# Layer norm split between VectorE and GpSimd, and the attention residual in two later step parts

## The chip, the cores and the metric

The kernel runs on one core of a Trainium2 chip. A core has five instruction streams: TensorE (PE in the profile, with its weight loads listed as PEld), VectorE (DVE), ScalarE (ACT), GpSimd (POOL) and SyncE (SP, which issues DMAs here). Each stream runs in its own order; between streams there are only semaphores. The metric is the device time of one execution in microseconds (us).

## The reference

Two rounds of an attention layer A and a gated feed-forward layer B, with the same weights in both rounds, on 2048 tokens of width 448.

```python
x = A_x
x = x + _A_ref(_layernorm(x), A_mem0, A_Wq, A_Wk, A_Wv, A_Wo, A_seg_len)
x = x + _B_ref(_layernorm(x), B_W_gate, B_W_up, B_W_down)
x = x + _A_ref(_layernorm(x), A_mem0, A_Wq, A_Wk, A_Wv, A_Wo, A_seg_len)
x = x + _B_ref(_layernorm(x), B_W_gate, B_W_up, B_W_down)

def _layernorm(x, eps=1e-05):
    return (x - mean(x)) / sqrt(var(x) + eps)
```

`_A_ref` walks the tokens in 64 segments of 32. Each segment attends, with 16 heads of 256, to 8 memory tokens and to itself; the attention's output for the memory tokens is the memory of the next segment, so the segments form a chain. `_B_ref` computes gate = x Wg (kept where positive), up = x Wu and (gate * up) Wd, with 1792 hidden columns.

## The kernel before

The weights are combined first: for each head, A holds Wq Wk^T and B holds Wv Wo, both kept on chip in bf16. Then come 72 steps and one closing step. In a step one segment of the first round (chain 0) and one segment of the second round (chain 1, 8 segments behind) are computed together, so that their 2 x 40 columns share PE's weight loads. A tile is 128 tokens, four segments; a block is four steps, and g mod 4 tells where in its block a step stands.

What a step does on PE, in the order of the code (`step`):

1. `project` for the first eight heads, the transposes of the input (`kps`), `project` for the other eight. Each product `prj` is copied out of PSUM by DVE or ACT into TQ or TZ.
2. Scores: `Sm` (memory rows) and `Sx` (segment rows) for both halves. `weights_of` makes the softmax, on DVE except for the exponential on ACT; its last result is PM or PX.
3. `fill(0)`, then `project_out` in pieces (`ox`), between them the transposes of PM and PX (`pps`, copied by DVE into PT) and the products `ya`, `yb` and `y` of those with the input, whose evacuations write Y.
4. `fill(1)` stands before the second half's `project_out`, `fill(2)` after `weigh_x(0)`, and `fill(3)` after `finish`, which copies the new memory into hT (DVE, `set_mem`) and the attention output into OT (ACT).

A `fill(k)` emits what the table `slots` holds for slot 4g + k. There the layer norms and the feed-forward are put. For block gb, with slot 16 gb + 16 as its zero:

- slot 3: `residual` for both tiles of the block (one of each round). It transposes OT on PE (`otp`), adds it to the tile in x_ring (line 341) and makes the layer norms of both tiles together.
- slots 4 to 12: the 21 units of the feed-forward: `xposed` (transposes of the normalised tiles, `tps`, evacuated into xT), 14 `gate_up` and six thirds of `down`. The last third for the first tile also starts that tile's next norm; the last third for the second tile stores the tile and reloads its place in x_ring, with DMAs on SP.
- slot 14: `prep_pe(1, ...)` writes the first tile into hT for round two.
- slots 4 and 6 also hold the next tile's norm for round one, `prep_ln`, and its `prep_pe`.

The order of PE's products and transposes is fixed as they are emitted (`in_order`). On the other engines a list scheduler orders the instructions of each engine when the program is built; on the chip each engine keeps that order.

A layer norm before (`rstd_nbias`, `layer_norm`): on DVE bn_stats, bn_aggr, three small operations for a seed of the inverse root (lines 261 to 266), three rounds of four operations of 128x1 or 128x2 (lines 270 to 274) that refine it, and one for the bias; on ACT one activation of 128x448 per tile (line 285); on POOL a copy of the last 64 columns (line 287), so that the tile has 512. Two tiles of one residual share the small operations.

Of the kernel before, what the change touches and what calls it, by code (L numbers as in the profile page):

```python
# [8 lines left out]
BF = mybir.dt.bfloat16  # L9
F32 = mybir.dt.float32  # L10
I32 = mybir.dt.int32
AF = mybir.ActivationFunctionType
ALU = mybir.AluOpType
AX = mybir.AxisListType

DM = 448
# [10 lines left out]
EPS = 1e-5  # L27
# [17 lines left out]
def build_kernel(ctx, tc, A_x, A_mem0, A_Wq, A_Wk, A_Wv, A_Wo, B_W_gate, B_W_up, B_W_down, out,  # L45
                 ntiles=16, nseg=64):
    nc = tc.nc
    P = nc.NUM_PARTITIONS
# [9 lines left out]
    psum = ctx.enter_context(tc.tile_pool(name="psum", bufs=7, space=bass.MemoryType.PSUM))  # L58
    p_ln = ctx.enter_context(tc.tile_pool(name="p_ln", bufs=2))
# [14 lines left out]
    def tr(*a):  # L74
        in_order(nc.tensor.transpose(*a))  # L75
# [10 lines left out]
    def xsl(t):  # L86
        return x_ring[:, t % R, :]
# [3 lines left out]
    ident = glob.tile([P, P], BF, name="ident")  # L91
# [7 lines left out]
                            op0=ALU.arith_shift_right, op1=ALU.bitwise_and)  # L99
    nc.vector.tensor_scalar(out=rowi[:, 2:3], in0=rowi[:, 0:1], scalar1=15, scalar2=None,  # L100
                            op0=ALU.bitwise_and)
# [9 lines left out]
    for b in range(4):  # L111
        o = 0 if b % 2 == 0 else MEM
        nc.vector.tensor_scalar(out=maskS[:, b, o:o + SEG], in0=keyf[:, b // 2, :], scalar1=rowf[:, 2:3],
                                scalar2=MASKVAL, op0=ALU.is_gt, op1=ALU.mult)
# [4 lines left out]
                            op0=ALU.mult, op1=ALU.add)  # L119
# [5 lines left out]
    for i in range(2):  # L125
        t = glob.tile([P, 4, HW], BF, name=f"hT{i}")
# [5 lines left out]
    with tc.tile_pool(name="pre", bufs=6) as pre:  # L132
# [4 lines left out]
        for i in range(6):  # L137
            t = pre.tile([P, 4, 512], BF, name=f"nat{i}", bufs=1)
# [111 lines left out]
        HK.append(t)  # L250


    def rstd_nbias(ts):
        n = len(ts)
        mv = p_ln.tile([P, 2, 2], F32, tag="ln_mv")
        for i, t in enumerate(ts):
            stats = p_ln.tile([P, nc.vector.BN_STATS_DIM], F32, tag="ln_stats")
            nc.vector.bn_stats(stats[:], xsl(t))
            nc.vector.bn_aggr(mv[:, i, :], stats[:])
        veps = p_ln.tile([P, 2], F32, tag="ln_veps", name="ln_veps")[:, 0:n]  # L260
        nc.vector.tensor_scalar(out=veps, in0=mv[:, 0:n, 1], scalar1=EPS, scalar2=None, op0=ALU.add)
        ti = p_ln.tile([P, 2], I32, tag="ln_ti", name="ln_ti")[:, 0:n]
        nc.vector.tensor_scalar(out=ti, in0=veps.bitcast(I32), scalar1=1, scalar2=None,
                                op0=ALU.arith_shift_right)
        rstd = p_ln.tile([P, 2], F32, tag="ln_rstd", name="ln_rstd")[:, 0:n]
        nc.vector.tensor_scalar(out=rstd.bitcast(I32), in0=ti, scalar1=-1, scalar2=0x5f3759df,
                                op0=ALU.mult, op1=ALU.add)
        tmp = p_ln.tile([P, 2], F32, tag="ln_tmp", name="ln_tmp")[:, 0:n]
        for _ in range(3):
            nc.vector.tensor_tensor(out=tmp, in0=rstd, in1=rstd, op=ALU.mult)  # L270
            nc.vector.tensor_tensor(out=tmp, in0=tmp, in1=veps, op=ALU.mult)
            nc.vector.tensor_scalar(out=tmp, in0=tmp, scalar1=-0.5, scalar2=1.5,
                                    op0=ALU.mult, op1=ALU.add)
            nc.vector.tensor_tensor(out=rstd, in0=rstd, in1=tmp, op=ALU.mult)
        nbias = p_ln.tile([P, 2], F32, tag="ln_nbias", name="ln_nbias")[:, 0:n]
        nc.vector.scalar_tensor_tensor(out=nbias, in0=mv[:, 0:n, 0], scalar=-1.0, in1=rstd,
                                       op0=ALU.mult, op1=ALU.mult)
        return rstd, nbias

    def layer_norm(ts):  # L280
        rstd, nbias = rstd_nbias(ts)
        xns = []
        for i, t in enumerate(ts):
            xn = p_ln.tile([P, 512], BF, tag="ln_xn", bufs=3)
            nc.scalar.activation(xn[:, 0:DM], xsl(t), AF.Identity,
                                 bias=nbias[:, i:i + 1], scale=rstd[:, i:i + 1])
            nc.gpsimd.tensor_copy(xn[:, DM:512], xn[:, 384:DM])
            xns.append(xn)
        return xns

    def transpose_tokens(xn):
        tps = psum.tile([P, 4, 128], BF, tag="ps", name="tps")
# [5 lines left out]
        return hTb[b % 2][:].rearrange("p s (i w) -> p s i w", w=HI)  # L298

    def prep_ln(t):  # L300
        return layer_norm([t])[0] if 0 <= t < ntiles else None

    def prep_pe(c, t, xn):

        if xn is None:
            return
        b = t + (LAG // 4 if c else 0)
        tps = transpose_tokens(xn)
        src = tps[:].rearrange("p k (s t) -> p k s t", t=SEG)
        h = chunks(b)  # L310
        x = slice(HX[c], HX[c] + SEG)
        nc.vector.tensor_copy(h[:, :, 0:4, x].transpose([0, 2, 1, 3]), src)
# [12 lines left out]
    def ffn_units(gb):  # L325

        tasks = []
        if gb < ntiles:
            tasks.append((0, gb))
        if 0 <= gb - LAG // 4 < ntiles:  # L330
            tasks.append((1, gb - LAG // 4))
        n2 = 128 * len(tasks)
        pr = Pair()

        def residual():
            for c, t in tasks:
                tp = psum.tile([P, 4, 128], BF, tag="ps", name="otp")
                for kd in range(4):
                    tr(tp[:, kd, :], OT[:, c, kd, :], ident[:])
                xt = xsl(t)  # L340
                nc.vector.tensor_tensor(xt, tp[:].rearrange("p k d -> p (k d)")[:, 0:DM], xt, op=ALU.add)
            pr.xns = layer_norm([t for _, t in tasks])

        def xposed():
            pr.xT = main.tile([P, 4, 256], BF, tag="xT", name="xT")
            pr.hh = main.tile([P, FT, 256], BF, tag="hh", name="hh")
            for i, xn in enumerate(pr.xns):
                tps = transpose_tokens(xn)
                evac(nc.scalar if i == 0 else nc.vector, pr.xT[:, :, 128 * i:128 * i + 128], tps[:])

        def gate_up(f):
            gps = psum.tile([P, 512], F32, tag="ps", name="gps")
            ups = psum.tile([P, 512], F32, tag="ps", name="ups")
            for W_sb, ps in ((Wu_sb, ups), (Wg_sb, gps)):
                for kd in range(4):
                    mm(ps[:, 0:n2], W_sb[:, kd, f * 128:(f + 1) * 128], pr.xT[:, kd, 0:n2],
                                     start=(kd == 0), stop=(kd == 3))
            ut = p_ut.tile([P, 256], BF, tag="ut")
            nc.scalar.copy(ut[:, 0:n2], ups[:, 0:n2])  # L359
            nc.vector.scalar_tensor_tensor(out=pr.hh[:, f, 0:n2], in0=gps[:, 0:n2], scalar=0.0,  # L360
                                           in1=ut[:, 0:n2], op0=ALU.max, op1=ALU.mult)

        def down(i, part):
            c, t = tasks[i]
            if part == 0:
                pr.dps = psum.tile([P, 512], F32, tag="ps", name="dps")
            f0, f1 = ((0, 5), (5, 10), (10, FT))[part]
            for f in range(f0, f1):
                mm(pr.dps[:, 0:DM], pr.hh[:, f, 128 * i:128 * i + 128], Wd_sb[:, f, :],
                                 start=(f == 0), stop=(f == FT - 1))  # L370
            if part < 2:
                return
            xt = xsl(t)
            nc.vector.tensor_tensor(xt, pr.dps[:, 0:DM], xt, op=ALU.add)  # L374
            if c == 1:
                nc.sync.dma_start(out_dram[t * 128:(t + 1) * 128, :], xt)
                if t + R < ntiles:
                    nc.sync.dma_start(xsl(t + R), x_dram[(t + R) * 128:(t + R + 1) * 128, :])

        def down_last(i):  # L380
            down(i, 2)
            if tasks[i][0] == 0:
                pr.xn2 = prep_ln(gb)

        units = [xposed] + [lambda f=f: gate_up(f) for f in range(FT)]
        for i in range(len(tasks)):
            units += [lambda i=i: down(i, 0), lambda i=i: down(i, 1), lambda i=i: down_last(i)]
        post = (lambda: prep_pe(1, gb, pr.xn2)) if gb < ntiles else None
        return residual, units, post


    def moving(hb, j, idx, chains):
# [201 lines left out]
    def at(s, fn):  # L594
        slots.setdefault(s, []).append(fn)

    for gb in range(nsteps // 4):
        residual, units, post = ffn_units(gb)
        s0 = 4 * (4 * gb + 4) + 3
        at(s0, residual)  # L600
        first, last = s0 + 1, s0 + 10
        for i, u in enumerate(units):
            at(first + (i * (last - first)) // len(units), u)
        if post is not None:
            at(last + 1, post)
        if gb + 1 < ntiles:
            sl = Pair()
            at(4 * (4 * gb + 1), lambda sl=sl, t=gb + 1: setattr(sl, "xn", prep_ln(t)))
            at(4 * (4 * gb + 1) + 2, lambda sl=sl, t=gb + 1: prep_pe(0, t, sl.xn))

    prep_pe(0, 0, prep_ln(0))
    set_mem(0, mem0T[:].unsqueeze(2), (0,))
# [66 lines left out]
```

## Time and profile before

| what | value |
|---|---|
| median of 3 runs (lowest, highest) | 1897.17 us (1897.12, 1898.62) |
| the profiled execution: its time | 1896.18 us |
| its span, first to last instruction | 1894.4 us |
| mean granted PE clock | 0.973 |
| line 258, DVE bn_stats, 128x448, x64 | 616 ns each |
| lines 270, 271, 272, 274, DVE, 128x1, x108 each | 158, 153, 149, 155 ns each |
| line 285, ACT activation, 128x448, x64 | 757 ns each |
| line 312, DVE copy into hT, 128x512 bf16, x32 | 413 ns each |
| line 341, DVE add of the residual, x32 | 386 ns each |

A line of the page's groups reads: source line, engine, operation, result and operands with their shapes and count, then busy us in total, mean ns of one, and the idle time of the engine just before such instructions with what ended it. A line of the timeline reads: start, length, engine, source line, operation, operands, count of merged instructions, and in brackets the idle time before and the instruction that ended it. Since matmuls are pipelined, an idle time of PE is a better measure of a wait than its busy share.

### The profile page before, as it was taken

How to read it: one execution, taken by the hardware profiler on the slowest of the kernel's cores; microseconds unless marked ns; L12 is line 12 of the kernel's file. 1: busy time of each engine (PE TensorE's matmuls, PEld its weight loads, DVE VectorE, ACT ScalarE, POOL GpSimd, SP SyncE). 2: the span in 40 equal slices, each digit the busy share in tenths (PEclk: the TensorE clock that was granted, in tenths of full speed). 3: DMA queues.
4: the chain of work that ended last, by engine and by line, in shares of the span. 5: the costliest groups of instructions: out<-in, count | busy, mean ns of one | idle time of the engine just before them, and what ended most of it. 6: DMA issues, size and time to landing. Idle time of an engine off the chain costs nothing. (4 is left out here: it accounts for less than half of the span.)

```text
span 1894.4 us, 91643 instructions
## 1 busy us (share of the span) xinstructions
PE 1762.2 (93%) x41570; PEld 1619.7 (86%) x41570; DVE 1183.9 (62%) x4637; ACT 733.6 (39%) x2139; POOL 45.7 (2%) x117
## 2 busy tenths in 40 slices
PE   6988989999999989899999989898999999998997
PEld 4578889889898989899898989898998989898887
DVE  5656676746666666656566656666466666666674
ACT  4634444433434333433334333343333343333332
POOL 2120000000000000000000000000000000000000
PEclk8989999999999999999999999999999999999999
DMA  6330000000000000000000000000000000000000
GB/s 203 122 104 5 4 4 3 3 3 8 3 8 3 8 3 8 3 3 9 3 8 3 8 3 8 3 3 8 3 8 3 8 3 5 3 6 3 6 4 8
DMA packets 20326, 29.04 MB, mean 15 GB/s; under 512 B 1496, under 2 KB 18272, under 8 KB 19936
## 3 DMA queue, kind: packets, MB, share of 16 engines
q1 hardware_dynamic: 18848, 19.50, 3.3%
q8 instruction: 325, 5.32, 1.1%
q0 software_dynamic: 1088, 3.68, 0.6%
q14 instruction: 65, 0.53, 0.1%
HBM read 21.34 MB, written 1.84 MB: 12 GB/s over the span
## 5 line engine op out<-in xcount | busy, mean ns | idle before, releaser
L72 PE MATMUL ox<-Y,B_sb 128*128 128x80 bf16 (+4 forms) x16352 | 610.8, 197 | 0.6 <-issue 0.3
L72 PEld LDWEIGHTS <-B_sb 128*128 128x128 bf16 x16352 | 589.3, 99 | 11.7 <-issue 1.0
L72 PE MATMUL prj<-hT,A_sb 128*128 128x80 bf16 (+1 forms) x16128 | 575.1, 197 | 5.5 <-DVE hT L319 3.7
L72 PEld LDWEIGHTS <-A_sb 128*128 128x128 bf16 x16128 | 555.3, 99 | 13.2 <-issue 5.9
L79 ACT CAST Y<-y 128x512 bf16<-128x512 f32 (+2 forms) x384 | 144.9, 412 | 244.4 <-PE y L72 180.2
L81 DVE CAST TQ<-prj 128x320 bf16<-128x320 f32 (+2 forms) x528 | 201.5, 392 | 49.9 <-PE prj L72 43.6
L81 DVE CAST Y<-y 128x128 bf16<-128x128 f32 (+2 forms) x384 | 161.4, 459 | 103.5 <-PE y L72 88.4
L79 ACT CAST TQ<-prj 128x320 bf16<-128x320 f32 (+2 forms) x528 | 176.0, 353 | 123.1 <-PE prj L72 109.4
L448 DVE COPY PT<-pps 128x128 bf16<-128x128 bf16 (+1 forms) x288 | 74.3, 258 | 190.4 <-PE pps L75 185.8
L72 PE MATMUL ups<-xT,Wu_sb 128*128 128x256 bf16 (+1 forms) x1008 | 149.2, 273 | 22.0 <-DVE xT L81 18.8
L360 DVE SCALAR_TENSOR_TENSOR hh<-gps,ut 128x256 bf16<-128x256 f32 (+1 forms) x252 | 98.9, 394 | 101.0 <-PE gps L72 60.1
L72 PE MATMUL gps<-xT,Wg_sb 128*128 128x256 bf16 (+1 forms) x1008 | 149.1, 273 | 0.0
L503 ACT CAST Y<-yb 128x192 bf16<-128x192 f32 x142 | 45.3, 319 | 262.2 <-PE yb L72 261.6
L359 ACT CAST ut<-ups 128x256 bf16<-128x256 f32 (+1 forms) x252 | 87.8, 349 | 122.2 <-PE ups L72 114.9
L72 PEld LDWEIGHTS <-hk 40*128 40x128 bf16 (+1 forms) x1990 | 101.6, 95 | 24.4 <-DVE x_ring L374 4.8
L72 PEld LDWEIGHTS <-Wu_sb 128*128 128x128 bf16 x1008 | 88.5, 102 | 39.1 <-DVE xT L81 22.0
L434 ACT ACTIVATE se<-se 128x80 f32<-128x80 f32 (+1 forms) x286 | 86.3, 303 | 62.9 <-DVE se L433 46.3
L72 PEld LDWEIGHTS <-Wg_sb 128*128 128x128 bf16 x1008 | 96.3, 103 | 13.0
L549 ACT CAST OT<-ox 128x128 bf16<-128x128 f32 x128 | 28.6, 269 | 182.5 <-DVE hT L319 177.1
L498 DVE CAST Y<-ya 128x256 bf16<-128x256 f32 x142 | 59.7, 420 | 57.4 <-PE ya L72 57.4
L72 PE MATMUL dps<-Wd_sb,hh 128*128 128x448 bf16 x448 | 92.7, 352 | 0.0
L72 PEld LDWEIGHTS <-TQ 128*128 128x128 bf16 x1962 | 89.2, 97 | 0.1
(112 smaller groups left out, 1892.2 us busy)
## 6 DMA issues: line engine op xcount, KB each, us to landing
wo<-in_A_Wo_dram POOLq DMA_DIRECT2D x8, 448.0 KB, 5.9
nat<-in_A_Wq_dram SPq DMA_DIRECT2D x8, 384.0 KB, 4.6
nat<-in_A_Wk_dram SPq DMA_DIRECT2D x8, 384.0 KB, 4.6
nat<-in_A_Wv_dram SPq DMA_DIRECT2D x8, 384.0 KB, 3.4
out_dram<-x_ring SPq DMA_DIRECT2D x16, 112.0 KB, 1.7
Wd_sb<-in_B_W_down_dram SPq DMA_DIRECT2D x1, 1568.0 KB, 14.7
x_ring<-in_A_x_dram SPq DMA_DIRECT2D x12, 112.0 KB, 2.0
Wg_sb<-in_B_W_gate_dram SPq DMA_DIRECT2D x1, 1344.0 KB, 6.4
```

The costliest lines, as they stand in the source:

```text
L72: in_order(nc.tensor.matmul(*a, **k))
L79: nc.scalar.copy(dst, src)
L81: eng.tensor_copy(dst, src)
L359: nc.scalar.copy(ut[:, 0:n2], ups[:, 0:n2])
L360: nc.vector.scalar_tensor_tensor(out=pr.hh[:, f, 0:n2], in0=gps[:, 0:n2], scalar=0.0, in1=ut[:, 0:n2], op0=ALU.max, op1=ALU.mult)
L434: nc.scalar.activation(se[:], se[:], AF.Exp, scale=SCALE)
L448: nc.vector.tensor_copy(PT[:], pps[:].rearrange("p b q -> p (b q)"))
L498: nc.vector.tensor_copy(YB[hf][:, 0:16, M0:M0 + 16], ya[:].rearrange("p (t q) -> p t q", q=16))
L503: nc.scalar.copy(YB[hf][:, 16:28, M0:M0 + 16], yb[:].rearrange("p (t q) -> p t q", q=16))
L549: nc.scalar.copy(OT[:, c, :, o:o + SEG], ox[:, :, XO[c]:XO[c] + SEG])
```

## The change

The layer norm is made for one tile at a time. The twelve refining operations are issued on GpSimd; bn_stats, bn_aggr and the seed stay on VectorE. The bias operation and ACT's activation go; VectorE writes (x - mean) * rstd in one tensor_scalar. `residual` becomes one function per tile, in slots 4 and 5 of the block (before: slot 3 for both). The 21 feed-forward units go to slots 7 to 12 (before: 4 to 12); slot 14 stays. The `prep_pe` of the next tile goes from slot 6 to slot 9.

```diff
-    def rstd_nbias(ts):
...
+    def layer_norm(t):
+        stats = p_ln.tile([P, nc.vector.BN_STATS_DIM], F32, tag="ln_stats")
+        nc.vector.bn_stats(stats[:], xsl(t))
+        mv = p_ln.tile([P, 2], F32, tag="ln_mv")
+        nc.vector.bn_aggr(mv[:], stats[:])
...
         for _ in range(3):
-            nc.vector.tensor_tensor(out=tmp, in0=rstd, in1=rstd, op=ALU.mult)
-            nc.vector.tensor_tensor(out=tmp, in0=tmp, in1=veps, op=ALU.mult)
-            nc.vector.tensor_scalar(out=tmp, in0=tmp, scalar1=-0.5, scalar2=1.5,
+            nc.gpsimd.tensor_tensor(out=tmp[:], in0=rstd[:], in1=rstd[:], op=ALU.mult)
+            nc.gpsimd.tensor_tensor(out=tmp[:], in0=tmp[:], in1=veps[:], op=ALU.mult)
+            nc.gpsimd.tensor_scalar(out=tmp[:], in0=tmp[:], scalar1=-0.5, scalar2=1.5,
                                     op0=ALU.mult, op1=ALU.add)
-            nc.vector.tensor_tensor(out=rstd, in0=rstd, in1=tmp, op=ALU.mult)
-        nbias = p_ln.tile([P, 2], F32, tag="ln_nbias", name="ln_nbias")[:, 0:n]
-        nc.vector.scalar_tensor_tensor(out=nbias, in0=mv[:, 0:n, 0], scalar=-1.0, in1=rstd,
-                                       op0=ALU.mult, op1=ALU.mult)
...
-            nc.scalar.activation(xn[:, 0:DM], xsl(t), AF.Identity,
-                                 bias=nbias[:, i:i + 1], scale=rstd[:, i:i + 1])
-            nc.gpsimd.tensor_copy(xn[:, DM:512], xn[:, 384:DM])
+            nc.gpsimd.tensor_tensor(out=rstd[:], in0=rstd[:], in1=tmp[:], op=ALU.mult)
+        xn = p_ln.tile([P, 512], BF, tag="ln_xn", bufs=3)
+        nc.vector.tensor_scalar(out=xn[:, 0:DM], in0=xsl(t), scalar1=mv[:, 0:1], scalar2=rstd[:],
+                                op0=ALU.subtract, op1=ALU.mult)
+        nc.gpsimd.tensor_copy(xn[:, DM:512], xn[:, 384:DM])
+        return xn
...
-        def residual():
-            for c, t in tasks:
+        pr.xns = []
+
+        def residual(i):
+            c, t = tasks[i]
...
-            pr.xns = layer_norm([t for _, t in tasks])
+            pr.xns.append(layer_norm(t))
...
-        residual, units, post = ffn_units(gb)
-        s0 = 4 * (4 * gb + 4) + 3
-        at(s0, residual)
-        first, last = s0 + 1, s0 + 10
+        residuals, units, post = ffn_units(gb)
+        s0 = 4 * (4 * gb + 5)
+        for i, r in enumerate(residuals):
+            at(s0 + i, r)
+        first, last = s0 + 3, s0 + 9
...
-            at(4 * (4 * gb + 1) + 2, lambda sl=sl, t=gb + 1: prep_pe(0, t, sl.xn))
+            at(4 * (4 * gb + 2) + 1, lambda sl=sl, t=gb + 1: prep_pe(0, t, sl.xn))
```

In the built program the order on VectorE in a step with g mod 4 = 1, from the transpose of PM[1] on, is this (operands shortened to names):

```
PT<-pps; ti; veps; rstd; ti; rstd; Y<-ya; xn (waits POOL); xn (waits POOL); PT<-pps;
x_ring<-otp; bn_stats; bn_aggr; veps; ti; rstd; Y<-y; Y<-y; xn (waits POOL); Y<-y; PT<-pps;
hT<-ox; xT<-tps; hh x3
```

and at the start of a step with g mod 4 = 3:

```
x_ring<-dps; Y; bn_stats; Y; bn_aggr; Y; veps; TZ; ti; TQ; rstd; TQ; xn (waits POOL); TQ; hk; TZ; TQ; mx<-Sm
```

More of the change, by code (lines that the diff above doesn't have):

```diff
@@ L250, in build_kernel @@
         HK.append(t)
-    def rstd_nbias(ts):
[L254 to L263, printed above, removed]
+    def layer_norm(t):
[3 more added lines that the diff above has]
+        nc.vector.bn_aggr(mv[:], stats[:])
+        veps = p_ln.tile([P, 1], F32, tag="ln_veps")
+        nc.vector.tensor_scalar(out=veps[:], in0=mv[:, 1:2], scalar1=EPS, scalar2=None, op0=ALU.add)
+        ti = p_ln.tile([P, 1], I32, tag="ln_ti")
+        nc.vector.tensor_scalar(out=ti[:], in0=veps[:].bitcast(I32), scalar1=1, scalar2=None,
@@ L264, in rstd_nbias @@
                                 op0=ALU.arith_shift_right)
-        rstd = p_ln.tile([P, 2], F32, tag="ln_rstd", name="ln_rstd")[:, 0:n]
-        nc.vector.tensor_scalar(out=rstd.bitcast(I32), in0=ti, scalar1=-1, scalar2=0x5f3759df,
+        rstd = p_ln.tile([P, 1], F32, tag="ln_rstd")
+        nc.vector.tensor_scalar(out=rstd[:].bitcast(I32), in0=ti[:], scalar1=-1, scalar2=0x5f3759df,
                                 op0=ALU.mult, op1=ALU.add)
-        tmp = p_ln.tile([P, 2], F32, tag="ln_tmp", name="ln_tmp")[:, 0:n]
+        tmp = p_ln.tile([P, 1], F32, tag="ln_tmp")
@@ L273, in rstd_nbias @@
                                     op0=ALU.mult, op1=ALU.add)
-            nc.vector.tensor_tensor(out=rstd, in0=rstd, in1=tmp, op=ALU.mult)
-        nbias = p_ln.tile([P, 2], F32, tag="ln_nbias", name="ln_nbias")[:, 0:n]
-        nc.vector.scalar_tensor_tensor(out=nbias, in0=mv[:, 0:n, 0], scalar=-1.0, in1=rstd,
-                                       op0=ALU.mult, op1=ALU.mult)
[L278 to L285, printed above, removed]
-                                 bias=nbias[:, i:i + 1], scale=rstd[:, i:i + 1])
-            nc.gpsimd.tensor_copy(xn[:, DM:512], xn[:, 384:DM])
-            xns.append(xn)
-        return xns
+            nc.gpsimd.tensor_tensor(out=rstd[:], in0=rstd[:], in1=tmp[:], op=ALU.mult)
@@ L300, in prep_ln @@
     def prep_ln(t):
-        return layer_norm([t])[0] if 0 <= t < ntiles else None
+        return layer_norm(t) if 0 <= t < ntiles else None
     def prep_pe(c, t, xn):
@@ L333, in ffn_units @@
         pr = Pair()
-        def residual():
-            for c, t in tasks:
[L337 to L341, printed above, removed]
-            pr.xns = layer_norm([t for _, t in tasks])
+        pr.xns = []
+        def residual(i):
+            c, t = tasks[i]
+            tp = psum.tile([P, 4, 128], BF, tag="ps", name="otp")
+            for kd in range(4):
+                tr(tp[:, kd, :], OT[:, c, kd, :], ident[:])
+            xt = xsl(t)
+            nc.vector.tensor_tensor(xt, tp[:].rearrange("p k d -> p (k d)")[:, 0:DM], xt, op=ALU.add)
+            pr.xns.append(layer_norm(t))
         def xposed():
@@ L388, in ffn_units @@
         post = (lambda: prep_pe(1, gb, pr.xn2)) if gb < ntiles else None
-        return residual, units, post
+        return [lambda i=i: residual(i) for i in range(len(tasks))], units, post
     def moving(hb, j, idx, chains):
```

## The prediction

> **What bounds the kernel now.** I read the page first, then PE's instructions in order of time over one block of four steps, then the granted clock step by step, then the rows of the small operations.
>
> ```profile
> PE 1762.2 (93%) x41570; PEld 1619.7 (86%) x41570; DVE 1183.9 (62%) x4637; ACT 733.6 (39%) x2139; POOL 45.7 (2%) x117
> ...
> PE pps L75 <- DVE PM L441: 58.6, 51, 2.3
> PE ups L72 <- DVE xT L81: 18.8, 14, 1.7
> PE otp L75 <- ACT OT L549: 10.7, 18, 0.6
> ```
>
> TensorE (PE) sets the end: nearly every microsecond in which it neither multiplies nor waits for an attention result is work that the change leaves as it is. So a change in time is a change in PE's idle time or in its clock. Its three recurring waits are listed (us in total, times, longest). In order of time they are these (start, length, idle before):
>
> ```profile
> 1204.05 0.62 PE L75 MATMUL otp<-ident,OT 128*128 128x128 bf16 x8 [0.62 <-ACT OT L549]
> ...
> 1216.02 0.23 PE L75 MATMUL pps<-ident,PM 128*128 128x128 bf16 x1 [2.30 <-DVE PM L441]
> ...
> 1219.63 1.03 PE L72 MATMUL ups<-xT,Wu_sb 128*128 128x256 bf16 x4 [1.18 <-DVE xT L81]
> ...
> 1301.59 0.23 PE L75 MATMUL pps<-ident,PM 128*128 128x128 bf16 x1 [0.80 <-DVE PM L441]
> ```
>
> I call a step class 0 to 3 by g mod 4. A block waits 0.62 (the residual's transposes) and 0.80 (second PM, nothing in between to do) in class 0, and 2.30 (first PM) and 1.18 (xT) in class 1: 4.90 us. The 2.30 is the layer norms' doing: on VectorE (DVE) the 30-odd small operations of the residual's and of the preparation's norm lie between the projection's evacuations. Classes 2 and 3 wait for nothing. The windows of two class-1 steps and of the next three (stretch, its length, PE, PEld, DVE, ACT, POOL busy, granted clock):
>
> ```profile
> 1000.49:1032.89 32.40, 28.48 (x620) 26.83 (x617) 19.87 (x85) 13.58 (x36) 0.71 (x3) 1.00 0.01 3
> 1209.17:1243.73 34.56, 31.09 (x620) 28.48 (x617) 19.87 (x85) 13.69 (x36) 0.71 (x3) 0.90 0.01 3
> 1243.73:1271.29 27.56, 27.56 (x595) 24.84 (x592) 16.83 (x65) 9.76 (x28) 0.00 (x0) 1.00 0.01 3
> 1271.29:1292.81 21.52, 21.52 (x549) 20.29 (x545) 14.23 (x51) 8.57 (x24) 0.24 (x1) 1.00 0.05 14
> 1292.81:1314.67 21.86, 20.44 (x543) 19.73 (x540) 14.60 (x56) 8.05 (x23) 0.00 (x0) 1.00 0.01 3
> ```
>
> The same class-1 work takes 32.40 us at full clock and 34.56 at 0.90: the idle cluster there also costs 2.16 us of clock, in 10 of some 14 such steps.
>
> **Part 1: the residual moves from the end of class 0 into class 1, split.** OT is then long ready, so the 0.62 goes. VectorE is no longer loaded during class 1's projection, so the 2.30 goes; steps of class 2 and 3, whose projections run without or with one norm, show none. No DMA moves: the store and the reload of x_ring stay in the slot of class 3 that holds the last down-projection, and SP's order is unchanged. The 21 feed-forward units go from nine slots into six, all in steps without idle, and PE's work is the same: nothing there. prep_pe three slots later has a whole step until its hT is read: nothing.
>
> **Part 2: Newton on GpSimd (POOL).** Twelve dependent operations of 128x1 per norm leave DVE. There each takes about 0.153 us, and one that waits for its forerunner starts 0.19 after it. POOL has no such row:
>
> ```profile
> L287 POOL COPY xn<-xn 128x64 bf16<-128x64 bf16 x64 | 15.3, 238 | 1773.7 <-ACT xn L285 1684.1 <-ACT TQ L79 89.2 <-PE prj L72 0.4
> L213 POOL COPY B_sb<-B_sb 128x192 bf16<-128x192 bf16 x16 | 5.6, 350 | 54.8 <-ACT B_sb L79 44.1 <-DVE B_sb L81 10.7
> L660 POOL MEMSET const-float32-0.0<- 128x1 f32 x1 | 0.1, 98 | 0.2 <-issue 0.2
> ```
>
> Call R the time from one operation of the chain to the next. Below: the 0.10 of a memset that reads nothing, and 0.06 for the handing over (ACT's xn ends at about 1213.48, two back to back in 1.41 from 1212.72, POOL starts at 1213.54): 0.16. Above: the 192-column copy, 0.35 and 0.06: 0.41. Between: the two copies differ by 112 ns for 128 columns, so a copy of one column would take 0.238 - 63 x 0.00088 = 0.18; with 0.06 and a little for the second input I take R = 0.25, so 3.0 us for a chain where DVE needed 12 x 0.19 = 2.3. Two chains side by side I price as one: copies on POOL start 0.28 apart at a length of 0.35, so they overlap.
>
> The skill speaks against this part: "GPSIMD Engine Reference", sections 3 and 4.1, puts ordinary elementwise work on VectorE and GpSimd at about twice its time, for two software dispatches. By that rule an operation would take 0.31, R 0.37, and the sum below would be 115 us instead of 41. No row of before tests it.
>
> **Part 3: normalising on VectorE.** ACT loses 64 activations of 0.757; it is 39% busy and nothing on the path waits for it in this: no gain but that wait's place. DVE gets one operation of 128x448 bf16; nearest row: the 128x512 copy into hT, 0.413, so I take 0.35 (bounds 0.2 and 0.6). What matters is the wait: this instruction sits in DVE's own order and waits for POOL. Behind it stand evacuations that PE needs. The built program's order on DVE gives three places per block.
>
> Class 1, walked from the first PM transpose as zero, with class 0 of before as the pattern (zero there 1297.19). PE: ox run from 1.43 + 0.23 (four transposes of the residual) over 2.17 to 3.83. DVE: PM[1] began at 4.11; now the residual's add (0.31 start to start) and one bn_stats (0.54) lie ahead of it, a reciprocal and a PX product (0.35) fall behind: 4.61, its transpose at 4.90. Idle 1.07.
> - Six operations (1.17) then precede the copy PT, which ends at 6.17: ya waits 0.25. PE comes to weigh_x(0) at 6.23 + 0.23 + 1.0 + 0.12 + 0.23 + 1.43 = 9.25.
> - First place: both norms' seeds are ready at 6.75, the chains end at 6.75 + 0.06 + 3.0 = 9.8. Then the second xn (the first is just ahead) and PT for PX[0], 0.29: 10.55. y starts at 10.6. Idle 1.35.
> - Second place: add, bn_stats, aggregate, three small ones: seed at 12.2; chain to 15.25; xn to 15.65; POOL's tail copy 0.24 and two handovers: 16.0. PE is at xposed's second transpose at 10.6 + 0.54 + 1.43 + 0.12 + 1.15 + 0.2 = 14.05. Idle 1.95. Behind xn on DVE stand Y, PT and the memory's hT (0.7), then xT at 16.4 to 16.8: the feed-forward's first product waits 0.65. This replaces the old 1.18.
> - Third place, class 3, zero its projection's start: the residual of the feed-forward, bn_stats and the seed, between evacuations, reach 3.1; chain to 6.1; xn to 6.45; then TQ, hk, TZ, TQ (1.5), so mx of Sm at 7.95 where a step without norms has it at 6.3. With the later evacuation already done in the gap, PM is at 9.6 and its transpose at 9.65 instead of 8.4. Idle 1.25, where there was none; before, the chain ran there on DVE itself and was done by 5.0.
>
> Class 0 keeps 0.80. **Sum:** 0.80 + 1.07 + 0.25 + 1.35 + 1.95 + 0.65 + 1.25 = 7.32 against 4.90: +2.4 us a block. Fourteen full blocks and three thin ones at the ends make 17 x 2.4 = 41. At the tail PE waits 5.28 for the last norm's xn; the chain's +0.7 there is met by 0.757 + 0.19 - 0.35 less: nothing. The first two norms' chains stand on POOL's queue ahead of its weight copies and the later four loads of Wo, where POOL idles 37 us before its first copy: nothing. Clock: pieces of at most 1.95 where 2.30 stood; I take a third of the cold steps off, -7. So 1896.18 + 41 - 7 = 1930 for the profiled execution, whose span of 1894.4 has 1.8 around it; the median of the runs is 1.0 above: **1931 us**.
>
> "TensorE: Matmul & The Clock Gate", Part 1, has the clock halve after an idle window of about 3.4 us. The 2.30 here already lowered it in most blocks and not in all, which the row alone shows. By the page no single wait of mine would trip it, and 15 us more would come off: 1916.
>
> **Rivals.**
> - Short links, faster. All three places move with R, 12 links each, 36R a block. At R = 0.16 the waits are 0.27, 0.87 and 0.17, the block 4.1: 17 x -0.8 = -14, and with the clock kept -22 more: 1860 to 1883. The point is R = 0.18 at equal clock, 0.22 if the clock stays full. For: POOL's memsets of 0.10. Against: they read nothing; copies of 0.24 do.
> - Long links: a two-input operation costs what the wide copies cost. At R = 0.35 the block gains 3.6 more, 17 x 6.0 = 102, and the waits pass 2.5, so the clock drops twice: some 2000 to 2020. For: the tail copy at 0.24 + 0.06 = 0.30 is already above mine. Against: 63 of its columns are not there.
> - The waits only change places: what class 1 loses and gains meets within 4 us: 1893 to 1901. It needs R near 0.2; nothing singles that out.
>
> That VectorE would not wait at all is excluded: xn needs rstd, and other work follows it in the built order.
>
> **How the numbers follow.** Forecast (slower by 4 to about 90 us) 0.55, long links 0.20, short links 0.20, no change 0.05. A measurement of this kernel tells 0.2%, 3.8 us. Faster 0.20, same 0.05, slower 0.75. Range: R from 0.18 with the clock kept (17 x -0.12 - 22 = -24: 1872) to 0.33 with a little clock (17 x 5.3 + 8 = 98: 1995). The likeliest case's own range is 1901 to 1985.
>
> **What would show it.** Right: PE's otp and first-PM waits gone; new PE waits in class 1 for PT of PX[0] and for xn, in class 3 for PM; DVE idle before xn, ended by POOL, 1 to 3 us each; POOL operations of 128x1 about 0.25 apart. Wrong: R far from 0.25, class 3 without idle, or class-1 steps all at clock 1.00.

## The result, and the profile after

The changed kernel takes 1928.47 us (median of 4 runs, 1926.05 to 1930.67) against 1897.2: a ratio of 1.0163, 95% interval 1.0145 to 1.0180. It is slower by about 31 us. Its profiled execution took 1930.67 us, 34.5 more than that of before; its span is 1928.8, its mean granted clock 0.975.

First the page of the changed kernel: engines' busy time, and the shares of the chain of waits that ended last.

```profile
PE 1774.2 (92%) x41570; PEld 1630.4 (85%) x41570; DVE 1146.6 (59%) x4093; ACT 696.1 (36%) x2075; POOL 179.4 (9%) x885
...
PE 70%; DVE 17%; POOL 7%; issue 3%; ACT 2%; DMA 1%; SPq 0%; ACTq 0%; DVEq 0%; POOLq 0%
```

VectorE lost 37 us of work and ScalarE 37; GpSimd got 134 and is still only 9% busy. But 7% of the chain that sets the end now runs through GpSimd: what counts is when its results come, not how busy it is. PE's waits of the changed kernel (waiting line, releaser; us in total, times, longest):

```profile
PE pps L75 <- DVE PM L432: 42.4, 52, 1.5
PE y L72 <- DVE PT L439: 30.9, 17, 2.1
PE tps L75 <- DVE xn L275: 22.1, 15, 5.6
PE Sm L72 <- DVE TQ L81: 12.0, 13, 0.9
PE ups L72 <- DVE xT L81: 7.3, 14, 0.5
```

The residual's wait for OT is gone, and PM costs 42.4 where it cost 58.6. New are the second, third and fourth lines: all end on VectorE, none on GpSimd. The waits in order of time, in one step of class 1 (start, length, instruction, in brackets the idle time of PE before it):

```profile
1233.44 0.23 PE L75 MATMUL pps<-ident,PM 128*128 128x128 bf16 x1 [0.83 <-DVE PM L432]
1239.67 0.62 PE L72 MATMUL y<-PT,hk 40*128 40x256 bf16 x10 [1.92 <-DVE PT L439]
1245.12 0.60 PE L75 MATMUL tps<-ident,xn 128*128 128x128 bf16 x4 [1.81 <-DVE xn L275]
1246.24 0.61 PE L72 MATMUL ups<-xT,Wu_sb 128*128 128x256 bf16 x4 [0.52 <-DVE xT L81]
```

Why VectorE is late is in its own timeline of that step:

```profile
1234.95 0.41 DVE L489 CAST Y<-ya 128x256 bf16<-128x256 f32 x1
1238.27 0.40 DVE L275 TENSOR_SCALAR xn<-x_ring,mv,rstd 128x448 bf16<-128x448 bf16 x1 [2.90 <-POOL rstd L273]
1239.02 0.40 DVE L275 TENSOR_SCALAR xn<-x_ring,mv,rstd 128x448 bf16<-128x448 bf16 x1 [0.36 <-POOL rstd L273]
1239.33 0.28 DVE L439 COPY PT<-pps 128x256 bf16<-128x256 bf16 x1
...
1244.67 0.40 DVE L275 TENSOR_SCALAR xn<-x_ring,mv,rstd 128x448 bf16<-128x448 bf16 x1 [2.38 <-POOL rstd L273]
```

VectorE stands still for 2.90 us in front of xn. The copy PT behind it has nothing to do with the norm, but it is what PE's y waits for: it ends at 1239.33 + 0.28 = 1239.61, and y starts 0.06 later. GpSimd's chain, same step (two interleaved chains, then a single one):

```profile
1235.41 0.19 POOL L271 TENSOR_SCALAR tmp<-tmp 128x1 f32<-128x1 f32 x1
1235.56 0.19 POOL L269 TENSOR_TENSOR tmp<-rstd 128x1 f32<-128x1 f32 x1
1235.71 0.19 POOL L273 TENSOR_TENSOR rstd<-rstd,tmp 128x1 f32<-128x1 f32 x1
...
1241.44 0.19 POOL L269 TENSOR_TENSOR tmp<-rstd 128x1 f32<-128x1 f32 x1 [1.66 <-DVE rstd L265]
1241.71 0.19 POOL L270 TENSOR_TENSOR tmp<-tmp,veps 128x1 f32<-128x1 f32 x1
1241.99 0.19 POOL L271 TENSOR_SCALAR tmp<-tmp 128x1 f32<-128x1 f32 x1
```

A link (from one operation of a chain to the next) takes 0.273 us in a single chain. Two chains share the engine at one operation per 0.145, so each advances by 0.29 a link: a pair takes 1234.87 to 1238.99, 4.1 us, where one chain takes 3.2. Most of the difference is the second chain's late start: its seed is ready at 1235.03, but in GpSimd's order three operations of the first chain stand ahead, and it begins at 1235.56.

In class 3 the same happens once. VectorE waits 2.91 us in front of xn, the copies into TQ come behind it, and PE's scores wait for one of them (two rows of VectorE, one of PE):

```profile
1287.77 0.40 DVE L275 TENSOR_SCALAR xn<-x_ring,mv,rstd 128x448 bf16<-128x448 bf16 x1 [2.91 <-POOL rstd L273]
1288.08 0.48 DVE L81 CAST TQ<-prj 128x320 bf16<-128x320 f32 x1
...
1288.71 0.20 PE L72 MATMUL Sm<-hT,TQ 128*128 128x80 bf16 x1 [0.92 <-DVE TQ L81]
```

The windows of a whole block, classes 0 to 3 (stretch, its length, busy time of PE, PEld, DVE, ACT, POOL, granted clock):

```profile
1203.84:1224.47 20.63, 19.83 (x536) 19.29 (x533) 12.88 (x45) 8.04 (x23) 0.00 (x0) 1.00 0.01 3
1224.47:1253.53 29.06, 23.95 (x575) 22.57 (x572) 18.36 (x69) 9.83 (x27) 6.72 (x39) 1.00 0.01 3
1253.53:1285.61 32.08, 32.08 (x642) 29.27 (x638) 18.12 (x62) 11.78 (x34) 0.76 (x4) 1.00 0.01 3
1285.61:1309.47 23.86, 22.80 (x553) 20.87 (x550) 14.00 (x48) 7.88 (x23) 1.76 (x9) 1.00 0.04 13
```

They sum to 105.63 us; the same block at full clock took 32.40 + 27.56 + 21.52 + 21.86 = 103.34 before, so it lost 2.29. PE's idle time in it (length less busy time) rose from 5.34 to 6.97, by 1.63; the other 0.66 is time in which PE counts as busy (98.00 before, 98.66 after). Class 2 carries 4.5 us more of the moved feed-forward and never waits; class 1 has five of the seven waits, class 3 one.

Where the 34.5 us of the two profiled executions lie, from both traces cut at the starts of steps 12 and 64 (half-clock: time in which PE's granted clock was 0.5):

| | before | after | difference | half-clock before, after |
|---|---|---|---|---|
| up to step 12 (weights, filling) | 347.8 | 357.2 | +9.4 | 27.3, 41.0 |
| steps 12 to 63, 13 full blocks | 1360.4 | 1374.9 | +14.5 | 61.4, 30.7 |
| steps 64 to 71 | 182.5 | 193.1 | +10.6 | 13.7, 23.9 |

Thirteen full blocks at 2.29 lost 29.8 us by waits; 14.5 came out, so the clock gave 15.3 back there. At the ends, which lost 20.0, the two can only be estimated apart. With half-clock time counted at one half, the clock took 11.9 there and the waits 8.1. But in the full blocks a stretch cost less than half of itself: before, the class-1 steps with 6.83 us of it were 2.0 to 2.3 longer than those at full clock; after, those with 3.41 were 0 to 1.3 longer. At the dearest of these, 1.33 for 3.41, the clock took 9.3 at the ends and the waits 10.7. By these two estimates the whole span has 38 to 41 us of waits, and -3 to -6 by the clock.

### The profile page after: what moved, and what is told of

Same layout as the page of the kernel before. It is cut to its first block, busy times and chain, and to the rows that moved or that the text cites. A ratio compares the mean times of both kernels' runs of the same rounds, so it can differ in the third digit from the quotient of the medians.

```text
span 1928.8 us, 91833 instructions
## 1 busy us (share of the span) xinstructions
PE 1774.2 (92%) x41570; PEld 1630.4 (85%) x41570; DVE 1146.6 (59%) x4093; ACT 696.1 (36%) x2075; POOL 179.4 (9%) x885
## 3 DMA queue, kind: packets, MB, share of 16 engines
HBM read 21.34 MB, written 1.84 MB: 12 GB/s over the span
## 4 chain that ended last, share of the span: by engine, by line
PE 70%; DVE 17%; POOL 7%; issue 3%; ACT 2%; DMA 1%; SPq 0%; ACTq 0%; DVEq 0%; POOLq 0%
PE prj L72 22%; PE ox L72 20%; PE ups L72 6%; PE gps L72 5%; PE dps L72 4%; PE y L72 3%; PE Sx L72 2%; DVE stats L256 2%; POOL tmp L271 2%; POOL tmp L269 2%; POOL tmp L270 2%; POOL rstd L273 2%; DVE ssum L427 2%; ACT se L425 2%; PE pps L75 1%
## 5 line engine op out<-in xcount | busy, mean ns | idle before, releaser
L72 PE MATMUL ox<-Y,B_sb 128*128 128x80 bf16 (+4 forms) x16352 | 620.4, 198 | 2.7 <-DVE Y L489 1.8
L269 POOL TENSOR_TENSOR tmp<-rstd 128x1 f32<-128x1 f32 x192 | 37.0, 193 | 1615.6 <-DVE rstd L265 864.1
L72 PE MATMUL ups<-xT,Wu_sb 128*128 128x256 bf16 (+1 forms) x1008 | 144.4, 268 | 10.6 <-DVE xT L81 7.3
L72 PE MATMUL gps<-xT,Wg_sb 128*128 128x256 bf16 (+1 forms) x1008 | 143.2, 266 | 0.0
L72 PE MATMUL y<-PT,hk 40*128 40x256 bf16 (+1 forms) x1280 | 90.1, 252 | 30.9 <-DVE PT L439 30.9
L275 DVE TENSOR_SCALAR xn<-x_ring,mv,rstd 128x448 bf16<-128x448 bf16 x64 | 25.3, 396 | 137.9 <-POOL rstd L273 137.9
```

The costliest lines, as they stand in the source:

```text
L72: in_order(nc.tensor.matmul(*a, **k))
L269: nc.gpsimd.tensor_tensor(out=tmp[:], in0=rstd[:], in1=rstd[:], op=ALU.mult)
```

## The experiments

The theory: GpSimd's chain costs the time, through xn in VectorE's order; the new slots gain a little. Rivals: the slots themselves cost; or normalising on VectorE costs; or the waits would be there with any engine and only change places. All ratios are to before, run on the same chip, with 95% intervals. "Block" is the mean block of steps 12 to 63 in the profiled execution, "idle" PE's idle time in it, "half" its half-clock time.

| run | median us | ratio | block | idle | half |
|---|---|---|---|---|---|
| before | 1897.2 | 1 | 104.65 | 4.97 | 4.73 |
| after | 1928.47 | 1.0163 (1.0145 to 1.0180) | 105.76 | 6.13 | 2.36 |
| e1_slots_only | 1895.59 | 0.9982 (0.9972 to 0.9991) | 104.34 | 5.03 | 2.10 |
| e2_norm_only | 1971.88 | 1.0381 (1.0365 to 1.0396) | 108.83 | 7.85 | 7.09 |
| e3_xn_on_pool | 1964.32 | 1.0339 (1.0321 to 1.0356) | 108.85 | 8.77 | 6.56 |
| e4_newton_dve | 1879.95 | 0.9902 (0.9884 to 0.9920) | 103.61 | 4.45 | 1.84 |
| e5_pool_2 | 1869.11 | 0.9852 (0.9836 to 0.9869) | 102.33 | 3.93 | 0 |
| e7_units_later | 1969.48 | 1.0376 (1.0360 to 1.0391) | 109.05 | 8.08 | 6.30 |
| e8_dve_later | 1886.08 | 0.9939 (0.9923 to 0.9956) | 103.95 | 5.01 | 1.58 |
| e9_both | 1851.44 | 0.9756 (0.9741 to 0.9770) | 101.40 | 3.78 | 0 |
| e10_both_pool | 1871.51 | 0.9867 (0.9852 to 0.9882) | 102.21 | 4.67 | 0 |
| e11_dve_2 | 1846.04 | 0.9729 (0.9715 to 0.9744) | 100.97 | 2.81 | 0 |
| e12_old_slots_dve | 1884.62 | 0.9933 (0.9917 to 0.9950) | 103.64 | 4.53 | 2.63 |
| e13_one_slot | 1931.98 | 1.0187 (1.0164 to 1.0210) | 106.11 | 6.87 | 2.10 |

**The slots alone.** The changed kernel with the old arithmetic (refining on VectorE, bias, activation on ScalarE), still one tile at a time.

```diff
-            nc.gpsimd.tensor_tensor(out=tmp[:], in0=rstd[:], in1=rstd[:], op=ALU.mult)
+            nc.vector.tensor_tensor(out=tmp[:], in0=rstd[:], in1=rstd[:], op=ALU.mult)
...
-        nc.vector.tensor_scalar(out=xn[:, 0:DM], in0=xsl(t), scalar1=mv[:, 0:1], scalar2=rstd[:],
-                                op0=ALU.subtract, op1=ALU.mult)
...
+        nc.scalar.activation(xn[:, 0:DM], xsl(t), AF.Identity, bias=nbias[:], scale=rstd[:])
```

> The changed kernel's slots with the layer norm of before (refining on VectorE, normalising on ScalarE), one tile at a time. Theory (VectorE waiting in its own order for GpSimd is what costs; the new slots by themselves gain): no instruction on VectorE waits for GpSimd, so PE's waits for PT of PX[0] (1.92 us in the changed kernel) and in class 3 (0.92) go; the wait for the second tile's xn stays, some 2.5, since 12 x 0.19 + 0.76 stand where 12 x 0.27 + 0.40 stood; the clock stays full in most blocks. Idle 4.6 a block against 5.3 before: 1860 to 1890 us. Rival (the later, denser slots are what costs): 1915 us or more.

It gained 0.2% and missed the 1860 to 1890 us that were expected: the clock still drops in 8 of the 13 full blocks. PE's waits of this run:

```profile
PE pps L75 <- DVE PM L434: 47.9, 65, 1.5
PE tps L75 <- ACT xn L278: 40.1, 16, 5.3
```

The 2.30 of the first PM went as foreseen (and y waits for nothing), but xposed now stands so soon after the second tile's norm that its transposes wait for ScalarE's xn, 2.5 us a block, as expected. The wait moved into another instruction: the slots are nearly neutral by themselves, which speaks against the first rival (the slots cost) and for a part of the third (waits change places).

**The norm alone**: the changed layer norm in the old slots (residuals of both tiles in one slot), as an edit of the changed kernel:

```diff
-        for i, r in enumerate(residuals):
-            at(s0 + i, r)
-        first, last = s0 + 3, s0 + 9
...
+        s0 = 4 * (4 * gb + 4) + 3
+        at(s0, residual)
+        first, last = s0 + 1, s0 + 10
```

> The slots of before with the changed layer norm. Theory: all norms' waits for GpSimd now lie in the projection of class 1, where VectorE's evacuations queue behind them: first PM about 4 us late where 2.30 stood, and about 1 in class 3; 1935 to 1965 us. Rival (the slots are what costs): 1889 to 1905 us, no more than before.

Right in direction, and 7 us above the expected range. Its waits of PE:

```profile
PE pps L75 <- DVE PM L430: 63.7, 51, 3.8
PE Sm L72 <- DVE mv L258: 28.0, 12, 2.3
```

VectorE in one class-1 step of the same run, at its projection:

```profile
1261.65 0.40 DVE L275 TENSOR_SCALAR xn<-x_ring,mv,rstd 128x448 bf16<-128x448 bf16 x1 [2.13 <-POOL rstd L273]
...
1268.41 0.40 DVE L275 TENSOR_SCALAR xn<-x_ring,mv,rstd 128x448 bf16<-128x448 bf16 x1 [2.79 <-POOL rstd L273]
1268.72 0.23 DVE L422 TENSOR_TENSOR se<-Sm,mx 128x80 f32<-128x80 f32 x1
```

In the old slots the norms fall into the projection of class 1, and xn stands there ahead of evacuations and of the softmax: the scores wait 2.3 a block (they waited for nothing before), PM up to 3.8, and the half-clock time rises to 7.1 us a block.

**Normalising on GpSimd too**, so that no xn stands in VectorE's order:

```diff
-        nc.vector.tensor_scalar(out=xn[:, 0:DM], in0=xsl(t), scalar1=mv[:, 0:1], scalar2=rstd[:],
+        nc.gpsimd.tensor_scalar(out=xn[:, 0:DM], in0=xsl(t), scalar1=mv[:, 0:1], scalar2=rstd[:],
```

> The changed kernel with the normalising operation on GpSimd too, so that neither VectorE nor ScalarE waits for GpSimd. Theory: the waits for PT of PX[0] and in class 3 go, the one for xn stays at 1.5 to 2.0; idle about 3.9 a block against 6.9: 1868 to 1895 us. Rival (the slots cost): 1915 us or more. Rival (GpSimd's work as such slows VectorE through shared access): little changes, 1915 to 1930 us, since GpSimd does more.

A miss, for a price that no row had shown. The group and PE's largest wait:

```profile
L275 POOL TENSOR_SCALAR xn<-x_ring,mv,rstd 128x448 bf16<-128x448 bf16 x64 | 119.0, 1860 | 5.2
```

```profile
PE tps L75 <- POOL xn L275: 101.9, 18, 7.2
```

GpSimd needs 1.86 us for what VectorE does in 0.40. The part that tests the mechanism held: the wait of y and that of class 3 are gone (class 3 has 0.00 idle), because nothing that waits for GpSimd stands ahead of those copies in VectorE's order. One wait is left there:

```profile
DVE mv L258 <- POOL xn L275: 34.2, 12, 2.9
```

It is the third norm's bn_aggr, which writes over a buffer of mv that GpSimd's xn still reads; the copy PT for y stands ahead of it. In place of the old waits xposed waits 6.8 us for xn itself, after three 1.86 and three chains on one engine. The expectation's other rival, that GpSimd's work as such slows VectorE, finds little here: VectorE's 128x320 copies into TQ took 0.49 us beside work of GpSimd and 0.49 without, bn_stats 0.63 and 0.61.

**Refining back on VectorE**, everything else as changed (the diff is the first pair of lines of the slots run, for all four operations):

> The changed kernel with the refining back on VectorE, normalising there too: one step of the change undone. Theory: as with the slots alone, with 0.40 in place of 0.76 on the last norm's way: idle about 4 a block, 1855 to 1885 us. Rival (VectorE's added normalising operations cost, not the wait): within 10 us of the changed kernel, above 1915 us.

1879.95: as the theory had it. Against the changed kernel the y wait is gone, class 3 has 0.28 instead of 1.06, tps still waits 2.03. The steps from before to after, by ratios times 1897.2: slots -3.4, normalising on VectorE instead of ScalarE -15.2, refining on GpSimd +49.5; sum +30.9. The second rival is excluded: in these slots normalising on VectorE is the change's best part.

**Two rounds instead of three**, on GpSimd. One of the three refining rounds of the inverse root is left out, so each chain has 8 links; it is no longer the same arithmetic.

```diff
-        for _ in range(3):
+        for _ in range(2):
```

> The changed kernel with two refining rounds on GpSimd in place of three: each chain has 8 operations, VectorE's order is the same. Theory (each place costs PE the length of the chain): four links of 0.273 us less for a single norm, eight operations of 0.145 less for the pair of class 1, so 1.92 falls by 1.2, 1.81 by 1.1, and the 1.06 of class 3 goes: 3.3 us a block, 1870 to 1895 us. Rival (it is the handing to another engine, not the chain's length): at most 10 us off, 1918 us or more.

1869.1, 59 us less than the changed kernel for four links of a chain and 1 under the expected range. The expectation's rival, that the handing over costs and not the length, allowed 10. Its waits of PE:

```profile
PE tps L75 <- DVE xn L275: 15.1, 15, 4.5
...
PE y L72 <- DVE PT L439: 11.9, 16, 1.0
```

In a steady block y fell from 1.92 to 0.76 (1.16 is four links of 0.29), tps from 1.81 to 0.72 (1.09 is four links of 0.273), class 3 from 1.06 to 0.13, and there is no half-clock time left in the full blocks; only xT waits 0.25 longer. All three places move with the chain's length, the first two one for one.

**Later units.** xposed one slot later, first with GpSimd, then with refining on VectorE, to see whether the remaining tps wait can be stepped around:

```diff
-        first, last = s0 + 3, s0 + 9
+        first, last = s0 + 4, s0 + 9
```

> The changed kernel with the feed-forward's units in slots 8 to 12 in place of 7 to 12, so that xposed stands a slot later than the second tile's norm. Theory: PE's wait for xn (1.81) goes and the one for PT of PX[0] stays at 1.92: 1.8 us a block less, 1888 to 1912 us. Rival (denser units cost): 1930 us or more.

> As the kernel with refining and normalising on VectorE, with the units in slots 8 to 12. Theory: its one large wait, 2.03 for xn at the end of class 1, goes, and with it the clock's drop there: 1832 to 1860 us. Rival (the wait moves to xT in class 2): 1870 to 1885 us.

Both missed; the second is 1 us above the range of its rival (xT waits instead, 1870 to 1885). The waits of PE in the first:

```profile
PE y L72 <- DVE PT L439: 46.6, 31, 2.4
...
PE ya L72 <- DVE PT L439: 24.6, 13, 1.9
PE ups L72 <- DVE xT L81: 22.7, 14, 1.7
```

and in the second:

```profile
PE ups L72 <- DVE xT L81: 22.7, 14, 1.7
PE prj L72 <- DVE hT L308: 14.4, 14, 3.7
PE y L72 <- DVE PT L439: 12.4, 14, 1.2
```

The tps wait goes and three others come: the y of the same step (0.9), xT at the start of class 2 (1.6, in both), and either the memory's hT (0.9) or, with GpSimd, a ya of class 3 (1.9) behind the chain of the next norm, which moved with the units. Here the third rival is right: VectorE has a fixed amount to do between the residual and xposed, and a later xposed only lets other instructions be late. With GpSimd it costs 41 us more than the changed kernel, with VectorE 6 more than without the step.

**A rearrangement.** Two rounds, refining on VectorE, units as above, the next tile's norm from slot 4 to 10 and its prep_pe from 9 to 13, the last three thirds of `down` in slot 16; then the same with refining on GpSimd:

```diff
+        early = units[:len(units) - 3] if len(units) > 18 else units
...
+        for u in units[len(early):]:
+            at(s0 + 12, u)
...
-            at(4 * (4 * gb + 1), lambda sl=sl, t=gb + 1: setattr(sl, "xn", prep_ln(t)))
+            at(4 * (4 * gb + 2) + 2, lambda sl=sl, t=gb + 1: setattr(sl, "xn", prep_ln(t)))
```

> As the one before, with two refining rounds, the next tile's norm moved from slot 4 to slot 10 (its prep_pe to slot 13), and the second tile's down-projection in slot 16, the first step part of the next class 0. Theory: PE's 0.80 in class 0 gets work in front of it, the 0.83 in class 1 shrinks; idle about 1.2 us a block against 2.2: 1812 to 1842 us. Rival (the products put in front delay what the next PM needs, or VectorE's later norms meet evacuations): no better than the one before.

> The fastest kernel so far (1851 us: later units, two refining rounds, the next tile's norm and one down-projection moved) with its refining on GpSimd. Theory (with chains of 8, and where PE has 1 us and more of work before it needs VectorE, the engine hardly matters): 1840 to 1865 us. Rival (GpSimd always costs more than VectorE): 1870 us or more.

The first fell short of its expectation, but fills the 0.80 of class 0 that all versions above have (class 0: 0.00 idle, 22.25 us); in its place class 2 waits 1.62 for xT. The second is 20 us slower and outside its expected range: the rival, that GpSimd always costs more, holds. Its y waits 1.69 where the first has 1.03, and class 3 waits 0.48.

**Two rounds on VectorE in the changed slots:**

> The changed kernel with two refining rounds, on VectorE. Theory: against three rounds on VectorE the wait for xn (2.03) falls by 4 x 0.19 and 0.28 in class 3 goes, 1 us a block: 1858 to 1872 us, so level with two rounds on GpSimd (1869). Rival (GpSimd costs at any length): 1850 us or less.

1846.0, the fastest of all, 2.7% under before, and 5 us under the rearrangement, which thus gained nothing: a block has 0.80, 0.83, 0.69 and 0.52 of idle left. The expected level with GpSimd's 1869 was missed; the rival, that GpSimd costs at any length, holds here too. PE's waits:

```profile
PE pps L75 <- DVE PM L432: 41.9, 52, 1.5
PE tps L75 <- DVE xn L275: 13.3, 14, 4.0
```

With two rounds GpSimd costs 23 us (1869.1 against 1846.0), with three 49 (1928.5 against 1880.0). The third round costs 59 on GpSimd and 34 on VectorE.

**Old slots, refining and normalising on VectorE:**

> The slots of before, refining and normalising on VectorE: the fourth corner of slots (old, new) by engine of the refining (VectorE 1880 and GpSimd 1928 in the new slots, GpSimd 1972 in the old). Theory: in class 1 the first PM is later than the 2.30 of before, by some 12 more small operations and three of 0.40: 1900 to 1925 us. If GpSimd's cost did not depend on the slots, this would be 1972 - 48 = 1924.

Faster than the 1900 to 1925 us expected: at full clock the first PM waits 1.54 instead of 2.30, xT 1.73 instead of 1.62, and half-clock time falls from 4.73 to 2.63 us a block. That fills a table of two by two, in us against before (ratio less one, times 1897.2; three rounds, normalising on VectorE):

| refining on | old slots | new slots |
|---|---|---|
| VectorE | -12.7 | -18.6 |
| GpSimd | +72.3 | +30.9 |

GpSimd costs 85 in the old slots and 49.5 in the new. The slots matter little with VectorE (6) and much with GpSimd (41): they are a cover for GpSimd's chain, and not enough of one.

**Both residuals in one slot** of the changed kernel, to test the split:

```diff
-            at(s0 + i, r)
+            at(s0, r)
```

> The changed kernel with both residuals in slot 4: the split undone. Theory: three chains share GpSimd in front of one place, 36 x 0.145 = 5.2 us in place of 3.5; PE's wait there grows by about 2.5, the one for xn (1.81) goes: 1935 to 1960 us. Rival (the split does nothing): 1920 to 1932 us.

```profile
PE y L72 <- DVE rstd L265: 34.0, 12, 3.0
PE Sm L72 <- DVE TQ L81: 12.0, 13, 0.9
PE ups L72 <- DVE xT L81: 11.5, 13, 1.7
PE ya L72 <- DVE PT L439: 10.3, 12, 0.9
```

By time the rival is right (+3.5 us, intervals overlapping), though the waits of PE, above, moved as the theory had it: tps no longer waits, y waits 2.8 instead of 1.9 and ya 0.9, and xT 1.7 in the blocks at full clock. Splitting the two tiles spreads the same loss over two places; it hardly lessens it.

## Why the prediction was right

**The mechanism** was that of the text: no wait of PE ends on GpSimd; xn waits in VectorE's order and holds PT and TQ, and PE waits for xn itself. Two rounds against three show that the waits follow the chain's length, and the run with xn on GpSimd shows that those of y and of class 3 end when no xn stands in VectorE's order. Not all of the new waits are GpSimd's: with refining on VectorE tps waits 2.03, xT the same 0.52 and class 3 still 0.28, so GpSimd's own places are y and most of class 3. And in class 3 PE stopped at the scores, for TQ (0.92), and only 0.14 at PM, which the text had named.

**The places and their sizes**, predicted against measured in a steady block: class 0 0.80 and 0.80, PM[1] 1.07 and 0.83, ya 0.25 and 0.06, y 1.35 and 1.92, tps 1.95 and 1.81, xT 0.65 and 0.52, class 3 1.25 and 1.06: 7.32 and 7.00. The 0.62 for OT and the 2.30 of the first PM went as said.

**The term that was mis-sized most is y.** "Two chains side by side I price as one" failed. From the second seed to the end of its chain it took 3.96 us (1235.03 to 1238.99), where the prediction had 3.05. Of the 0.91 more, 0.47 is the second chain's late start behind the first (0.53 after its seed, where 0.06 was taken), 0.24 the sharing (3.43 for its links, 3.19 for a chain alone) and 0.19 the price of the links. The seeds came 0.57 earlier than walked, 6.18 after the first PM transpose, and hid a part of it.

**R** is 0.273 where 0.25 was taken, inside its bounds of 0.16 and 0.41. The memset of 0.10 was the wrong end; the interpolated copy (0.18 for one column) was near the operation's 0.19. The Trainium skill's "GPSIMD Engine Reference", section 4.1, puts two-input elementwise work on GpSimd at about twice VectorE's time. Here line 273 on 128x1 takes 0.189 us against 0.157 in the run with refining on VectorE, 1.2 times, and a dependent link 0.273 against 0.19, 1.4 times. By the rule the sum was 115 us; the waits cost about 40. For tiles this small the measurement decides.

**The sum of waits** was 41; estimated as above it came to 38 to 41. The full blocks lost 2.29 each, where 2.4 was forecast; the ends some 8 to 11, where four times 2.4 would be 9.7. That the 2.4 fits is in part luck. The 4.90 it starts from is a block with its clock lowered. At full clock a block waited 5.34 before, since xT then cost 1.62 and not 1.18 (in the row 1000.49:1032.89 PE is idle for 32.40 - 28.48 = 3.92, not 3.48). The idle time rose by 1.63; the 0.66 by which PE's busy time grew was not in the sum.

**The clock** was put at -7 and gave -3 to -6. "A third of the cold steps off" was wrong in kind: nine class-1 steps of the full blocks had a lowered clock before and nine after, but each for 3.41 us instead of 6.83. Of the 30.7 us of half-clock time that went there 23.9 came back at the filling and the draining, where it rose from 41.0 to 64.9. The prediction priced the thin blocks at their waits alone. +34 was forecast for the profiled execution and +34.5 measured; that they agree so closely is luck: the 2.4 a block and the -7 both rest on terms that came out otherwise, and no run shows how waits and clock share the ends.

**The rivals.** Short links needed R at 0.18 or 0.22; long links 0.35. Neither occurred: 0.273 lies between. "The waits only change places" was wrong for the change, but right for each attempt to move units.

**What was costed at nothing** is mostly confirmed: class 2 has no wait with 4.5 us more work, ScalarE's lost work shows nowhere; the tail's wait for the last xn grew from 5.28 to 5.63. One was not nothing: with the slots moved, tps waited for ScalarE's xn (2.46 us in a block, 2.03 with xn on VectorE), and normalising on VectorE was worth 15 us in all.

## What to carry to other kernels

Before an operation goes to a less busy engine, ask who waits for its result and what stands behind that waiting instruction: a dependent chain there costs its latency, link by link, however idle the engine. When the wait sits in an in-order engine that also empties PSUM, unrelated products pay for it; of two chains on one engine the second can start late, behind what the engine's order puts ahead of it. The largest single remedy was fewer links (59 us); the change with refining left on VectorE and two rounds is faster (1846) than either kernel, while moving the consumer later only made something else late.

## What the runs showed of the hardware

**A clock that drops on a raster.** The half-clock stretches of the changed kernel from step 13 to 49 (step, start in the span, start within the step, length), from its granted clock:

```
13   398.86  21.04  3.413
17   501.26  16.49  3.413
21   607.07  16.67  3.413
25   712.88  16.85  3.413
29   818.70  17.03  3.413
49  1351.18  21.08  3.413
```

All starts are multiples of 3.413 us apart (30, 31, 31, 31 and 156 times). A block of 105.64 is 0.17 us less than 31 of these, so the start moves on by 0.17 to 0.18 a block. In step 17 the raster's window before the drop, 13.08 to 16.49, holds the whole y wait of 1.92; in step 33, where the drop would fall at 16.96, 0.27 of that wait lies outside, in the window before, and there is no drop. Steps 33 to 45 have the same waits at full clock. So which blocks drop is partly a matter of phase, not of the wait's length alone. What counts seems to be PE's idle time summed within one window: in the full blocks the nine drops follow windows with 1.77 to 2.30 us of it, and the fullest windows of the four blocks without a drop hold 1.66, 1.71, 1.81 and 1.81. It is no full rule, since 1.77 dropped (step 25) and 1.81 did not (steps 41 and 45). The Trainium skill's "TensorE: Matmul & The Clock Gate", Part 1, describes a free-running window of about 3.4 us, which this raster shows; its drop after an idle window is not what is seen, since no wait in these steps fills more than 1.92 us of one. A drop can also cost nothing: step 17 takes 29.07 us with it, step 45 29.07 without, since PE's slower work ends inside the tps wait.

**GpSimd's prices**: 0.19 us for an operation of 128x1, 0.273 a dependent link, 0.145 an operation when two chains interleave, but 1.86 us for a 128x448 tensor_scalar with a mean and a scale per partition, 4.7 times VectorE's 0.396. The one operation of the pair that ran beside VectorE's xn took 0.25 instead of 0.19, in twelve of the thirteen full blocks; whether the two share something was not tried.
